# Attention and a gated MLP on one core: products with v per key block, and another set of planner numbers

## The chip, the cores and the metric

The kernel runs on one core of a Trainium2 chip. The metric is the device time of one execution in microseconds (us). Lower is better. The engines are named as in the profile: PE (TensorE; PEld is its weight load), DVE (VectorE), ACT (ScalarE), POOL (GpSimd) and SP (SyncE, which here only issues DMAs).

## The reference

Attention over 8 batches, 8 heads, 576 positions and 64 features per head, with rotary embedding of q and k; then a gated MLP over each batch. All inputs and outputs are float32.

```python
q_rot, k_rot = rotate(q), rotate(k)
scores = (q_rot @ k_rot.T) / sqrt(64)
attn = exp(scores - max(scores)); attn /= sum(attn) + 1e-9
x = heads_joined(attn @ v)                       # (8, 576, 512)
h = relu(x @ w_in)                               # w_in 512 x 1024
u, vv = h[..., :512], h[..., 512:]
vn = (vv - mean(vv)) / sqrt(var(vv) + 1e-6)
vs = w_spatial @ vn + b_spatial                  # w_spatial 576 x 576
out = (u * vs) @ w_out                           # w_out 512 x 512
```

## The kernel before, in words

**The work.** A pair is two heads of one batch; there are 32 pairs, four to a batch. After the fourth pair of a batch, the MLP of that batch is entered. `attention_plain` (pairs 0 to 3) and `attention` (the other 28) have the same steps. For each of nine score tiles, `scores` multiplies on PE into PSUM (tile sc), takes the negated row maximum on DVE (tile nmx, L615) and the exponential with its row sum on ACT (tile e, L617). Two PSUM slots hold the score tiles, so the third tile waits until the exponential of the first has read its slot. `values_plain` and `values` then transpose the exponentials on PE in blocks of 128 keys (tile tp), copy them out of PSUM, and multiply by v into the PSUM tile pv. Pairs 0 to 3 copy plain float32 (tile et, either on ACT at L701 or on DVE at L703) and multiply in float32. From pair 4 on, ACT takes the rounded high part (eh, L645) and DVE the rest (el, L358), and both parts are multiplied. `normalise` takes the reciprocals of the row sums on DVE, sends them through DRAM by DMA (tiles rt and rb), multiplies the output x32 by them, and splits it in a high and a low part (tile x) for the MLP.

**Preparing a pair.** `prepare` loads q and k of a pair (tile st), rotates them (L453, L457), splits them (L446, L449 for q), and copies the parts by DMA into the layouts that the score products read (qs, ks, qz, lk).

**Weights.** The MLP's weights arrive as 64-bit words and `decode` turns each of the 12 blocks of 512 KB into a high and a low float32 part: a DMA, six DVE instructions (L390 twice, L396, L398, L399, L358) and two ACT instructions. `spatial` splits the spatial weights (wsp).

**The MLP.** `mlp` has four products on PE: pa (x by the second half of w_in), pb (x by the first half), pc (the spatial product), pd (the output). pa needs the x of all four pairs of its batch and the blocks wi10 to wi13.

**What sets the order.** Nothing is issued directly. Each instruction, or a few that belong together, is an `op` with an engine, an assumed duration, and a key. `Program.run` plays the program through once, at build time: when an engine is free, it takes the op with the lowest key whose inputs are there and whose buffers (numbered slots) are free. So the keys decide the order on each engine, and on the chip every engine then works through its list in that order; a wait of the first instruction holds up all that stand behind it. `SLOTS` gives three PSUM slots (pm) to the transposed blocks, the decode and the MLP's products together.

- `pair_op` gives an op that POOL can do also to DVE when its key is below `EARLY`. `STEAL` is added to the key on the second engine of an op that has two.
- `UNTIL` is the key up to which ACT, DVE and POOL wait for a more urgent op that will soon be ready.
- `warm` puts a product of zeros on PE (tile warm, a filler) where the plan leaves PE idle. After the planned time `WARM_FULL` (ns) this is done only when PE has been idle for `WARM_AFTER` ns.
- `DEC_V`, `DEC_S`, `DEC_U`, `DEC_O` are the keys of the weight blocks; `PREP_E`, `PREP_AT`, `PLAIN_E`, `PLAIN_AT`, `S_AT2`, `NORM_E` shift the keys of the first six pairs; `MOE0` sets those of the first batch's MLP.

**The products with v of pairs 0 to 3.** `values_plain` has two parts: c = 0 takes three tiles of query rows of both heads, c = 1 the rest. In each there are five key blocks kt. `GROUPS2` says which key blocks share one op on PE: 0 and 1, 2 and 3, then 4 for c = 0; 0 and 1, then 2 to 4 for c = 1.

Of the kernel before, what the change touches and what calls it, by code (L numbers as in the profile page):

```python
# [17 lines left out]
P = 128  # L18
# [18 lines left out]
}  # L37
PSUM = {"sc": 1024, "pv": 512, "pm": 512}
MOE_START, MOE_LENGTH = 92.26, 81.46
DEC_V = [61.0, 61.37, 51.29, 10.34]  # L40
DEC_S = [-41.87, 45.71, 53.32]
DEC_U = [38.89, 69.87, 96.53, 99.39]
DEC_ON = 11.04
DEC_O = [84.23, 50.01, 188.95, 101.97]

CHUNKS = [
# [33 lines left out]
PLAIN_E = [-3.79, 8.57, 7.67, 12.33, 3.82]  # L80
PLAIN_AT = [-3.92, -2.03, -14.17, -18.58]
NORM_E = [42.54, 29.37, 43.65, 15.11, 31.49]
MOE0 = [92.68, 81.44]
# [7 lines left out]
def act_ns(n):  # L91
    return 51 + n * 5 // 6
# [29 lines left out]
class Program:  # L122
# [5 lines left out]
    def op(self, eng, ns, key, f, r=(), w=(), new=(), port=False, late=0):  # L128
        return self.either({eng: ns}, key, lambda e: f(), r, w, new, port, late)
# [139 lines left out]
def tile_attention_gated_mlp(  # L269
# [33 lines left out]
    op = prog.op  # L303
# [251 lines left out]
    def attention_plain(i):  # L555
# [122 lines left out]
    def values_plain(i, c, pieces, pairs_e, e1, vr, x32, key):  # L678

        pv = Buf("pv", None, None, f"pv{i}_{c}")  # L680
        whole_e = [(e, j) for e in pairs_e for j in range(2)] + ([(e1, 0), (e1, 1)] if e1 else [])
        nq = 384 if c == 0 else 192
        K_HI, K_AV, K_HALF = PLAIN_E[2:]
        held = chain[-1:]
        chain.append(f"{i}_{c}")

        def turned(at, name, blocks):

            tp = Buf("pm", None, None, f"tp{name}")
            et = Buf("eh", [P, CW], F32, f"et{name}")  # L690

            def transpose():
                for m, b in enumerate(blocks()):
                    nc.tensor.transpose(out=tp[:, m * P:m * P + P], in_=b, identity=ident)

            n = len(blocks.__defaults__[0])
            op(PE, 110 * n, at, transpose, r=["ident", *whole_e, *([] if name.endswith("_0a") else held)], w=[tp], new=[tp])

            def evacuate(e):
                if e == ACT:  # L700
                    nc.scalar.activation(et[:, :n * P], tp[:, :n * P], AF.Copy)  # L701
                else:
                    nc.vector.tensor_copy(out=et[:, :n * P], in_=tp[:, :n * P])  # L703

            last = [chain[-1]] if name.endswith(f"_{NQ - 1}") else []
            prog.either({ACT: act_ns(n * P), DVE: dve_ns(n * P)}, at + K_HI, evacuate, r=[tp, *held], w=[et, *last], new=[et], port=False)
            return et

        def block(kt):

            at = key + KT_STEP2[c] * kt
            name = f"{i}_{c}_{kt}"
            k0, k1 = kt * P, S + TW + kt * P
            if kt < 4 and c == 0:
                ea = turned(at, name + "a", lambda es=pairs_e, k0=k0: [e[:, k0:k0 + P] for e in es])
                eb = turned(at + 0.1, name + "b", lambda es=pairs_e, k1=k1: [e[:, k1:k1 + P] for e in es])
                return [(ea, 0, 0, P, 0, 384), (eb, 1, 0, P, 0, 384)]
            if kt < 4:
                et = turned(at, name, lambda es=[(pairs_e[0], k0), (e1, k0), (pairs_e[0], k1)]: [e[:, k:k + P] for e, k in es])
                return [(et, 0, 0, P, 0, 192), (et, 1, 0, P, 192, 192)]  # L720
            if c == 0:
                et = turned(at, name, lambda es=pairs_e: [e[:, 4 * P:5 * P] for e in es])
                return [(et, 0, 0, TW, 0, 384), (et, 1, TW, P, 0, 384)]
            et = turned(at, name, lambda es=[pairs_e[0], e1]: [es[0][:, 4 * P:5 * P], es[1][:, 4 * P:]])
            return [(et, 0, 0, TW, 0, 192), (et, 1, TW, P, None, 192)]

        for group in GROUPS2[c]:
            parts = [(kt, *part) for kt in group for part in block(kt)]

            def multiply(parts=parts):  # L730
                for kt, et, h, r0, r1, c0, n in parts:
                    out = pv[64 * h:64 * h + 64, :n]
                    cols = [(out, et[r0:r1, c0:c0 + n])] if c0 is not None else [(out[:, :TW], et[r0:r1, P + TW:2 * P]), (out[:, TW:], et[r0:r1, :P])]
                    for m, (dst, rhs) in enumerate(cols):
                        nc.tensor.matmul(dst, lhsT=vr[r0:r1, kt, h, :], rhs=rhs, start=(kt == 0 and m == 0), stop=(kt == 4 and m == len(cols) - 1))
# [297 lines left out]
```

## Time and profile before

| | |
|---|---|
| runs of the kernel | 953.69, 955.63 and 3209.75 us; median 955.63 us |
| profiled execution | 953.54 us, span 951.7 us |
| busy share of the span | PE 98%, DVE 72%, ACT 79%, POOL 60% |
| PE idle, 0 to 160 us of the span | 14.7 us |
| PE idle, 160 to 280 us | 0.12 us |
| fillers on PE | 71, the last before 110 us |

The run of 3209.75 us is over three times the other two and is not a time of this program's work. The profiled execution agrees with the other two. The shares are means over the whole span: the kernel has a start in which PE waits, and a long part in which it does not.

### The profile page before, as it was taken

Reading aid. Unit: us, or ns where it says so; the run is one execution under the profiler, and the core shown is the slowest. Engines: PE = TensorE matmul, PEld = TensorE weight load, DVE = VectorE, ACT = ScalarE, POOL = GpSimd, SP = SyncE. Lnnn points to the kernel's source line nnn. Section 1 sums busy time; section 2 is a strip of 40 time slices with the busy share of each in tenths; the row PEclk is TensorE's granted clock in tenths of the full one; section 3 lists DMA queues with packets and bytes.
Section 4 is the critical chain, followed back from the end, with each engine's and each line's share of the span. In section 5 each row is a group of like instructions: output and inputs, shape, how many; then the busy total and the mean of one; then the engine's idle time right before and its main releaser. Section 6 shows DMA issues by size and latency. Waiting matters only on the chain.

```text
span 951.7 us, 19634 instructions
## 1 busy us (share of the span) xinstructions
PE 932.9 (98%) x6685; PEld 858.7 (90%) x6685; DVE 683.5 (72%) x1477; ACT 749.9 (79%) x1853; POOL 566.9 (60%) x495
## 2 busy tenths in 40 slices
PE   8999899999999999999999999999999999999998
PEld 4656689999899999999899998999999998999998
DVE  6899887776877678766877668676787767766331
ACT  4989789778987789877897779877898778976452
POOL 7766556655766647776575756656576665752131
PEclk9999999999999999999999999999999999999999
DMA  9787454554454554346355445446544455430101
GB/s 332 228 236 199 131 133 113 139 156 112 122 133 114 160 155 110 103 118 173 115 141 138 99 148 126 122 130 165 126 115 117 128 147 154 103 67 13 64 1 51
DMA packets 57382, 124.65 MB, mean 131 GB/s; under 512 B 13249, under 2 KB 15169, under 8 KB 57282
## 3 DMA queue, kind: packets, MB, share of 16 engines
q1 hardware_dynamic: 56594, 122.73, 47.4%
q8 instruction: 53, 0.87, 0.4%
q10 hardware_dynamic: 688, 0.66, 0.2%
q14 instruction: 47, 0.39, 0.1%
HBM read 66.03 MB, written 9.58 MB: 79 GB/s over the span
## 4 chain that ended last, share of the span: by engine, by line
PE 71%; ACT 12%; DMA 5%; POOL 4%; DVE 3%; issue 3%; SPq 1%; POOLq 0%; DVEq 0%; ACTq 0%
PE pc L849 13%; PE sc L591 12%; PE pv L658 11%; PE pd L867 11%; PE tp L634 10%; PE pb L831 7%; PE pa L808 5%; ACT e L617 3%; ACT eh L645 3%; POOL st L453 2%; SPq L352 1%; DMA vr<-in_v_dram 1%; ACT avt L675 1%; POOL st L457 1%; DMA st<-in_qk_dram 1%
## 5 line engine op out<-in xcount | busy, mean ns | idle before, releaser
L358 DVE TENSOR_TENSOR el<-tp,eh 128x384 fp32r<-128x384 f32 x336 | 185.7, 555 | 128.2 <-ACT eh L645 120.6
L645 ACT ACTIVATE eh<-tp 128x384 fp32r<-128x384 f32 (+1 forms) x504 | 217.2, 433 | 68.2 <-PE tp L634 61.7
L617 ACT ACTIVATE e<-sc,nmx 128x576 f32<-128x576 f32 x288 | 213.1, 741 | 41.5 <-DVE nmx L615 39.1
L615 DVE TENSOR_REDUCE nmx<-sc 128x1 f32<-128x576 f32 x288 | 214.6, 749 | 23.6 <-PE sc L591 18.9
L453 POOL TENSOR_TENSOR st<-st,tabs 128x576 f32<-128x576 f32 x122 | 172.7, 1440 | 70.5 <-DMA st<-in_qk_dram 28.5
L634 PE MATMUL tp<-ident,e 128*128 128x128 f32 (+1 forms) x1176 | 197.8, 273 | 4.2 <-DVE el L358 3.6
L634 PEld LDWEIGHTS tp<-ident,e 128*128 128x128 f32 (+1 forms) x1176 | 146.6, 138 | 17.8 <-DVE el L358 6.3
L658 PE MATMUL pv<-eh,vs 128*128 128x384 f32 (+1 forms) x560 | 147.7, 305 | 0.0
L831 PE MATMUL pb<-x,wi 128*128 128x288 f32 x768 | 145.9, 308 | 0.6 <-DVE el L358 0.2
L849 PE MATMUL pc<-wsp,vn 128*128 128x288 f32 x768 | 145.5, 306 | 0.0
L867 PE MATMUL pd<-g,wo 128*128 128x288 f32 x744 | 138.5, 305 | 0.0
L591 PE MATMUL sc<-ks,qs 128*128 128x288 f32 x620 | 135.6, 308 | 2.4 <-ACT e L617 2.2
L808 PE MATMUL pa<-wi,x 128*128 128x512 f32 x448 | 132.9, 407 | 0.0
L591 PE MATMUL sc<-lk,qz 128*128 128x288 f32 x558 | 119.8, 296 | 0.0
L831 PEld LDWEIGHTS pb<-x,wi 128*128 128x128 f32 x768 | 113.2, 189 | 5.8 <-DVE el L358 2.1
L849 PEld LDWEIGHTS pc<-wsp,vn 128*128 128x128 f32 x768 | 113.2, 189 | 1.2
L658 PE MATMUL pv<-el,vs 128*64 128x384 f32 (+1 forms) x448 | 114.0, 295 | 0.0
L867 PEld LDWEIGHTS pd<-g,wo 128*128 128x128 f32 x744 | 109.6, 189 | 2.2 <-PE pc L849 0.2
L591 PEld LDWEIGHTS sc<-ks,qs 128*128 128x128 f32 x620 | 98.4, 189 | 11.8 <-ACT e L617 6.4
L658 PEld LDWEIGHTS pv<-eh,vs 128*128 128x128 f32 x560 | 98.7, 188 | 4.5
L358 POOL TENSOR_TENSOR g<-u,g 128x288 fp32r<-128x288 f32 x64 | 51.7, 815 | 72.9 <-ACT g L355 72.9
L457 POOL TENSOR_TENSOR st<-st 128x576 f32<-128x576 f32 x62 | 88.6, 1433 | 1.3
(170 smaller groups left out, 1433.0 us busy)
## 6 DMA issues: line engine op xcount, KB each, us to landing
st<-in_qk_dram SPq DMA_DIRECT2D x62, 576.0 KB
ks<-st SPq DMA_DIRECT2D x124, 160.0 KB
qs<-st SPq DMA_DIRECT2D x124, 144.0 KB
vr<-in_v_dram SPq DMA_DIRECT2D x32, 320.0 KB
qz<-st SPq DMA_DIRECT2D x62, 144.0 KB
out_dram<-ob SPq DMA_DIRECT2D x31, 288.0 KB
ws<-in_w_spT_dram SPq DMA_DIRECT2D x2, 576.0 KB
st<-in_qk_dram SPq DMA_DIRECT2D x2, 288.0 KB
```

Of the source, the lines that this page charges most:

```text
L358: eng.tensor_tensor(out=lo, in0=src, in1=hi.bitcast(F32), op=ALU.subtract)
L453: f = lambda e: e.tensor_tensor(out=st[j][:, cols], in0=st[j][:, cols], in1=tabs[:, cols], op=ALU.mult)
L591: nc.tensor.matmul(pt[:, c * 512:c * 512 + HALF], lhsT=lhsT, rhs=rhs[:, k0 + c * HALF:k0 + (c + 1) * HALF], start=(n == 0), stop=(n == len ...
L615: op(DVE, 665, key + k_max, lambda: nc.vector.tensor_reduce(out=nmx.tile, in_=tops(), op=ALU.max, axis=AX.XY, negate=True), r=[pt], w=[nmx ...
L617: op(ACT, 730, key + k_exp, lambda: nc.scalar.activation(e[:, e0:e0 + S].rearrange("p (c n) -> p c n", c=2), tops(), AF.Exp, bias=nmx.tile ...
L634: nc.tensor.transpose(out=tp[:e.shape[1], m * P:m * P + P], in_=e, identity=ident)
L645: nc.scalar.activation(h, p, AF.Copy)
L658: nc.tensor.matmul(pv[0:rows, c1:c2], lhsT=vs[:, kt, h, vp, :], rhs=part[:, c1:c2], start=(kt == 0 and n == 0 and c1 == 0), stop=last)
L808: nc.tensor.matmul(pm.tile, lhsT=lhsT, rhs=win[1, d][:, j, :], start=(d == 0 and n == 0), stop=(d == 3 and n == len(todo) - 1))
L831: nc.tensor.matmul(pm[:, :HALF], lhsT=win[0, d][:, i, f * P:(f + 1) * P], rhs=x[d][:, at:at + HALF], start=(d == 0 and n == 0), stop=(d == ...
L849: nc.tensor.matmul(pm[:, :HALF], lhsT=lhsT, rhs=rhs, start=(t == 0 and n == 0), stop=(t == 4 and n == 1))
L867: nc.tensor.matmul(pm[:, :HALF], lhsT=wout[d,][:, i, m * P:(m + 1) * P], rhs=gs[d][:, at:at + HALF], start=(d == 0 and n == 0), stop=(d == ...
```

## The change

Each key block of `values_plain` becomes an op of its own: `GROUPS2` goes, and the products with v of one kt stand as one entry in PE's list. All keys of the first six pairs, of the weight blocks and of the first MLP are replaced by others, and `EARLY`, `STEAL`, `UNTIL` and the numbers of the fillers too. The instructions of the real work are the same ones: PE has 1176 transposes of the split path, 164 plain transposes and 84 products with v in pairs 0 to 3 in both programs. The fillers go from 71 to 57.

```diff
-DEC_V = [61.0, 61.37, 51.29, 10.34]
+DEC_V = [26.55, 56.08, 48.79, 40.85]
...
-GROUPS2 = [[[0, 1], [2, 3], [4]], [[0, 1], [2, 3, 4]]]
...
-EARLY = 120
-STEAL = 48.41
-WARM_FROM, WARM_FULL, WARM_TO, WARM_NS, WARM_AFTER, WARM_COLS = 2500, 41589.04, 100000, 170, -242.78, 384
+EARLY = 98.54
+STEAL = 18.43
+WARM_FROM, WARM_FULL, WARM_TO, WARM_NS, WARM_AFTER, WARM_COLS = 2500, 32000, 100000, 170, 250, 384
...
-UNTIL = 88.1
+UNTIL = 37.27
...
-PREP_E = [22.66, -9.84, 10.25, 18.9, 53.04, 5.96, 15.45, 5.12, 9.56, -8.37]
-PREP_AT = [-30.48, 14.73, -2.52, -5.21, 7.85, -3.35]
+PREP_E = [27, 8, 8, 9, 9, 11, 30, 8, -2, -9]
+PREP_AT = [0, 0, 0, 0, 0, 0]
...
-        for group in GROUPS2[c]:
-            parts = [(kt, *part) for kt in group for part in block(kt)]
-
-            def multiply(parts=parts):
-                for kt, et, h, r0, r1, c0, n in parts:
+            def multiply(kt=kt, parts=parts):
+                for et, h, r0, r1, c0, n in parts:
...
-            op(PE, len(group) * nq * 39 // 20 + 360, key + KT_STEP2[c] * group[-1] + K_AV, multiply, r=[vr, *dict.fromkeys(part[1] for part in parts)], w=[pv], new=[pv] if group[0] == 0 else [])
+            op(PE, nq * 21 // 11 + 90, at + K_AV, multiply, r=[vr, *dict.fromkeys(p[0] for p in parts)], w=[pv], new=[pv] if kt == 0 else [])
```

The numbers in a row below are the program's buffer names: nmx0_0_1 is the maximum of pair 0, head 0, tile 1, tp1_0_2a a transposed block of pair 1, c = 0, kt = 2; the last number only counts buffers.

The first place is DVE's list at the start: the last steps of rotating q of pair 0 (st0_0) and the first maxima. Before:

```order
L532 SCALAR_TENSOR_TENSOR st0_0_103<-st0_0_103,tabs_63 128x2x384
L615 TENSOR_REDUCE nmx0_0_0_179<-sc0_0_0_153 128x1
L615 TENSOR_REDUCE nmx0_1_0_187<-sc0_1_0_173 128x1
L390 TENSOR_SCALAR dcwi13_200<-wi13raw_155 128x512
L516 TENSOR_TENSOR st0_0_103<-st0_0_103 128x384
L396 SCALAR_TENSOR_TENSOR sgwi13_225<-wi13raw_155,dcwi13_200 128x512
L390 TENSOR_SCALAR dcwi13_200<-wi13raw_155 128x512
L615 TENSOR_REDUCE nmx0_0_1_236<-sc0_0_1_227 128x1
```

And now:

```order
L531 SCALAR_TENSOR_TENSOR st0_0_103<-st0_0_103,tabs_63 128x2x384
L515 TENSOR_TENSOR st0_0_103<-st0_0_103 128x384
L614 TENSOR_REDUCE nmx0_0_0_177<-sc0_0_0_153 128x1
L614 TENSOR_REDUCE nmx0_1_0_185<-sc0_1_0_171 128x1
L452 TENSOR_TENSOR st1_0_134<-st1_0_134,tabs_63 128x576 x2
L614 TENSOR_REDUCE nmx0_0_1_214<-sc0_0_1_205 128x1
```

The addition that ends the rotation of q (L516, now L515) no longer stands behind the first decode step of a weight block; the first decode step of any block (wi10) now comes as row 22 of DVE's list, after seven maxima and two copies.

The second place is DVE's list where pair 4, the first of the split path, begins. Before:

```order
L358 TENSOR_TENSOR wo2_1416<-dcwo2_1299,wo2_1416 128x512
L615 TENSOR_REDUCE nmx4_1_0_1442<-sc4_1_0_1428 128x1
L358 TENSOR_TENSOR el4_0_0_1456<-tp4_0_0_1421,eh4_0_0_1433 128x384
L358 TENSOR_TENSOR el4_0_1_1464<-tp4_0_1_1435,eh4_0_1_1453 128x384
L615 TENSOR_REDUCE nmx4_0_4_1466<-sc4_0_4_1446 128x1
L453 TENSOR_TENSOR st5_1_1334<-st5_1_1334,tabs_63 128x576
L358 TENSOR_TENSOR x3_1477<-x32_3_1323,x3_1477 128x576
L358 TENSOR_TENSOR x3_1477<-x32_3_1323,x3_1477 128x64
L358 TENSOR_TENSOR el4_0_2_1501<-tp4_0_2_1468,eh4_0_2_1489 128x384
L358 TENSOR_TENSOR el4_0_3_1504<-tp4_0_3_1473,eh4_0_3_1493 128x384
```

And now:

```order
L357 TENSOR_TENSOR el4_0_0_1421<-tp4_0_0_1390,eh4_0_0_1405 128x384
L357 TENSOR_TENSOR el4_0_1_1427<-tp4_0_1_1396,eh4_0_1_1409 128x384
L614 TENSOR_REDUCE nmx4_1_1_1435<-sc4_1_1_1411 128x1
L769 TENSOR_TENSOR x32_3_1326<-x32_3_1326,rb3_1360 128x576
L357 TENSOR_TENSOR wo3_1442<-dcwo3_1300,wo3_1442 128x512
L357 TENSOR_TENSOR el4_0_2_1462<-tp4_0_2_1437,eh4_0_2_1450 128x384
L357 TENSOR_TENSOR x3_1464<-x32_3_1326,x3_1464 128x576
L357 TENSOR_TENSOR x3_1464<-x32_3_1326,x3_1464 128x64
L448 SCALAR_TENSOR_TENSOR st6_0_1322<-st6_0_1322 128x576
L357 TENSOR_TENSOR el4_0_3_1492<-tp4_0_3_1466,eh4_0_3_1483 128x384
```

The block el4_0_0 was row 147 of DVE's list, after all 72 decode steps; it is row 140 now, after 65 of them: the last step of wo3 and all six of wo2 come later. Of the work that DVE shares with POOL, st4_0, st5_1, x2, x3 and x4 stood on DVE before; now st1_0, one piece of wsp, x32_3 and x3. The low part of x3 stood ahead of el4_0_2 and stands behind it now; a multiplication of x32_3, which waits for the DMA of rb3, stands ahead of it.

The third place is PE's list in pair 1. Before:

```order
L735 MATMUL pv1_0_660<-et1_0_0a_599,vr1_221 64x384
L735 MATMUL pv1_0_660<-et1_0_0b_606,vr1_221 64x384
L735 MATMUL pv1_0_660<-et1_0_1a_640,vr1_221 64x384
L735 MATMUL pv1_0_660<-et1_0_1b_642,vr1_221 64x384
L694 MATMUL tp1_0_3a_682<-ident_64,e2_1_0_523 128x128
```

And now:

```order
L731 MATMUL pv1_0_602<-et1_0_0a_557,vr1_174 64x384
L731 MATMUL pv1_0_602<-et1_0_0b_567,vr1_174 64x384
L693 MATMUL tp1_0_2a_614<-ident_64,e2_1_0_444 128x128
L693 MATMUL tp1_0_2a_614<-ident_64,e2_1_1_407 128x128
L693 MATMUL tp1_0_2a_614<-ident_64,e2_1_2_472 128x128
L693 MATMUL tp1_0_2b_618<-ident_64,e2_1_0_444 128x128
L693 MATMUL tp1_0_2b_618<-ident_64,e2_1_1_407 128x128
L693 MATMUL tp1_0_2b_618<-ident_64,e2_1_2_472 128x128
L731 MATMUL pv1_0_602<-et1_0_1a_594,vr1_174 64x384
L731 MATMUL pv1_0_602<-et1_0_1b_606,vr1_174 64x384
```

The products with v are cut by transposes after every key block instead of every second one. Over pairs 0 to 3 the unbroken runs of such products go from 20 to 34. From the middle of pair 10 on (its score tile of head 1, tile 0), PE's list is the same in both programs up to the end: the last 2541 rows.

More of the change, by code (lines that the diff above doesn't have):

```diff
@@ L39 @@
 MOE_START, MOE_LENGTH = 92.26, 81.46
-DEC_V = [61.0, 61.37, 51.29, 10.34]
[L41 to L44, printed above, removed]
+DEC_V = [26.55, 56.08, 48.79, 40.85]
+DEC_S = [13.58, 17.95, 35.36]
+DEC_U = [60.17, 42.39, 60.35, 107.48]
+DEC_ON = 6.04
+DEC_O = [78.92, 112.46, 208.15, 120.91]
 CHUNKS = [
@@ L60 @@
 ]
-S_AT2 = [[0.99, 10.82, -7.22, 13.5, 0.81, 1.57], [19.07, 23.53, 32.12]]
-GROUPS2 = [[[0, 1], [2, 3], [4]], [[0, 1], [2, 3, 4]]]
-KT_STEP2 = [2.15, 2.61]
-VALUES_AT2 = [10.98, 25.07]
-EARLY = 120
-STEAL = 48.41
-WARM_FROM, WARM_FULL, WARM_TO, WARM_NS, WARM_AFTER, WARM_COLS = 2500, 41589.04, 100000, 170, -242.78, 384
+S_AT2 = [[1.7, 4.65, -0.43, 6.89, 3.7, 8.06], [10.81, 19.68, 16.79]]
+KT_STEP2 = [1.84, 0.43]
+VALUES_AT2 = [13.48, 26.26]
+EARLY = 98.54
+STEAL = 18.43
+WARM_FROM, WARM_FULL, WARM_TO, WARM_NS, WARM_AFTER, WARM_COLS = 2500, 32000, 100000, 170, 250, 384
 PATIENT = (DVE, ACT, POOL)
-UNTIL = 88.1
+UNTIL = 37.27
 LATE_LOAD = 2200
@@ L77 @@
 PREP = [30.19, 35.32, -8.17, -24.92, 16.24, 1.9, 50.58, 22.5, 37.15, -9.46]
-PREP_E = [22.66, -9.84, 10.25, 18.9, 53.04, 5.96, 15.45, 5.12, 9.56, -8.37]
-PREP_AT = [-30.48, 14.73, -2.52, -5.21, 7.85, -3.35]
[L80 to L83, printed above, removed]
+PREP_E = [27, 8, 8, 9, 9, 11, 30, 8, -2, -9]
+PREP_AT = [0, 0, 0, 0, 0, 0]
+PLAIN_E = [1.25, 4, 1.0, 4.0, 3.0]
+PLAIN_AT = [0, 0, 0, 0]
+NORM_E = [15, 21, 26, 24, 27]
+MOE0 = [90, 82]
 K_NORM, K_RELU, K_GATE, K_GHI, K_GLO, K_OB, K_OUT = 28.57, -7.71, 10.98, 19.59, 15.51, -9.41, -27.84
@@ L707, in turned @@
             return et
-        def block(kt):
+        for kt in range(NQ):
             at = key + KT_STEP2[c] * kt
@@ L716, in block @@
                 eb = turned(at + 0.1, name + "b", lambda es=pairs_e, k1=k1: [e[:, k1:k1 + P] for e in es])
-                return [(ea, 0, 0, P, 0, 384), (eb, 1, 0, P, 0, 384)]
-            if kt < 4:
+                parts = [(ea, 0, 0, P, 0, 384), (eb, 1, 0, P, 0, 384)]
+            elif kt < 4:
                 et = turned(at, name, lambda es=[(pairs_e[0], k0), (e1, k0), (pairs_e[0], k1)]: [e[:, k:k + P] for e, k in es])
-                return [(et, 0, 0, P, 0, 192), (et, 1, 0, P, 192, 192)]
-            if c == 0:
+                parts = [(et, 0, 0, P, 0, 192), (et, 1, 0, P, 192, 192)]
+            elif c == 0:
                 et = turned(at, name, lambda es=pairs_e: [e[:, 4 * P:5 * P] for e in es])
-                return [(et, 0, 0, TW, 0, 384), (et, 1, TW, P, 0, 384)]
-            et = turned(at, name, lambda es=[pairs_e[0], e1]: [es[0][:, 4 * P:5 * P], es[1][:, 4 * P:]])
-            return [(et, 0, 0, TW, 0, 192), (et, 1, TW, P, None, 192)]
-        for group in GROUPS2[c]:
-            parts = [(kt, *part) for kt in group for part in block(kt)]
-            def multiply(parts=parts):
-                for kt, et, h, r0, r1, c0, n in parts:
+                parts = [(et, 0, 0, TW, 0, 384), (et, 1, TW, P, 0, 384)]
+            else:
+                et = turned(at, name, lambda es=[pairs_e[0], e1]: [es[0][:, 4 * P:5 * P], es[1][:, 4 * P:]])
+                parts = [(et, 0, 0, TW, 0, 192), (et, 1, TW, P, None, 192)]
+            def multiply(kt=kt, parts=parts):
+                for et, h, r0, r1, c0, n in parts:
                     out = pv[64 * h:64 * h + 64, :n]
```

## The prediction

> **What bounds the kernel now.** I read the page's head first, then the windows of the span, then the fillers alone.
>
> ```profile
> span 951.7 us, 19634 instructions
> PE 932.9 (98%) x6685; PEld 858.7 (90%) x6685; DVE 683.5 (72%) x1477; ACT 749.9 (79%) x1853; POOL 566.9 (60%) x495
> ```
>
> PE is busy for 98%, but this mean covers two stages. The windows give, for each stretch, its length, the busy time of PE, PEld, DVE, ACT and POOL, PE's granted clock, and the DMA share:
>
> ```profile
> 0.00:30.00 30.00, 25.76 (x124) 13.75 (x124) 20.57 (x34) 15.73 (x36) 19.12 (x30) 1.00 0.87 297
> 30.00:103.67 73.67, 67.62 (x466) 46.25 (x467) 69.95 (x113) 67.08 (x165) 50.40 (x42) 1.00 0.79 225
> 103.67:107.60 3.93, 3.83 (x24) 2.97 (x22) 3.75 (x6) 3.56 (x10) 3.71 (x4) 1.00 0.88 272
> 107.60:111.00 3.40, 0.00 (x0) 0.00 (x0) 3.40 (x4) 0.00 (x0) 3.40 (x3) 0.99 0.02 3
> 111.00:114.00 3.00, 2.91 (x12) 2.69 (x13) 2.20 (x6) 1.50 (x4) 0.85 (x1) 0.50 0.00 0
> 114.00:137.80 23.80, 23.60 (x147) 20.55 (x146) 20.61 (x55) 20.62 (x54) 11.26 (x9) 0.99 0.45 115
> 137.80:160.00 22.20, 21.62 (x162) 20.17 (x162) 18.00 (x41) 21.00 (x54) 15.87 (x13) 1.00 0.58 146
> 160.00:280.00 120.00, 119.88 (x882) 114.44 (x881) 87.54 (x192) 99.01 (x247) 76.25 (x65) 1.00 0.47 124
> 280.00:952.00 672.00, 667.70 (x4879) 637.89 (x4877) 457.46 (x1032) 521.41 (x1292) 386.08 (x335) 1.00 0.43 115
> ```
>
> From 160 to 280 us PE is idle for 0.12 us: it is the bound. Both programs share their order from the middle of pair 10 on; 1666 matmuls stand ahead of that point, and the windows up to 280 us count 1817. So the change can move the end only by what it does to the start. There PE is idle for 4.24 + 6.05 + 0.10 + 3.40 + 0.09 + 0.20 + 0.58 = 14.7 us, and DVE for only 3.7 us of the 73.67 up to 103.67: DVE sets the pace there (95% busy), with ACT behind it (91%).
>
> ```profile
> 0.00:30.00 30.00, 12.26 (x55) 1.00 0.87 297
> 30.00:110.00 80.00, 5.23 (x16) 1.00 0.77 221
> ```
>
> These are the fillers alone: 55 before 30 us, 16 after. All work on PE is the same after the change, so the time is the span less what the start loses. A gain of 2% would be 19 us. The start offers 14.7 us of idle time plus the fillers, and most of the first 14 us is waiting for the first data, so I rule a gain of that size out almost wholly.
>
> **The first score tiles.** Rows of DVE, PE and, from the chain of waits, a DMA:
>
> ```profile
> 8.76 0.95 DVE L532 SCALAR_TENSOR_TENSOR st<-st,tabs 128x768 f32<-128x768 f32 x1
> 12.42 0.69 DVE L390 TENSOR_SCALAR dcwi<-wi13raw 128x512 int32<-128x512 int32 x1 [1.01 <-PE warm L941]
> 13.02 0.89 DVE L516 TENSOR_TENSOR st<-st 128x384 f32<-128x384 f32 x1
> 22.04 0.76 DVE L615 TENSOR_REDUCE nmx<-sc 128x1 f32<-128x576 f32 x1 [0.56 <-PE sc L601]
> 103.67 0.55 DVE L358 TENSOR_TENSOR el<-tp,eh 128x384 fp32r<-128x384 f32 x1
> 9.20 1.24 PE L601 MATMUL sc<-kf,st 64*128 64x288 f32 x6
> 10.37 2.61 PE L941 MATMUL warm<-zero 128*128 128x384 bf16 x15
> 14.06 2.18 PE L601 MATMUL sc<-kf,st 64*128 64x288 f32 x8 [1.08 <-DVE st L516]
> 4.83 7.49 DMA wi13raw<-in_w_in_dram
> ```
>
> Weight block wi13 lands at 4.83 + 7.49 = 12.32 us. The decode step L390 waits for it, and the addition L516 stands behind that step though its own input was there at 8.76 + 0.95 = 9.71. PE's third score tile waits for L516 and begins at 14.06. After the change the addition comes directly behind L532 and ends near 10.6. PE then has its second tile (until 9.20 + 1.24 = 10.44) and nine fillers of 2.61 / 15 = 0.174 us in front of the third: 10.44 + 1.57 = 12.0. That is 2 us sooner.
>
> **DVE's list up to pair 4.** The row at 22.04 is the seventh maximum; el4_0_0 begins at 103.67. Between them stand 123 rows of the order (24 to 146), so one takes 81.63 / 123 = 0.664 us, waits included. Afterwards seven maxima are done by row 19, 2 us sooner (20.0), then two copies, then rows 22 to 139: 118 rows. Prices of one maximum, decode step and copy:
>
> ```profile
> L615 DVE TENSOR_REDUCE nmx<-sc 128x1 f32<-128x576 f32 x35 | 25.8, 752 | 2.8 <-PE sc L591 1.4 <-PE sc L601 1.1
> L399 DVE SCALAR_TENSOR_TENSOR dcwi<-dcwi,sgwi 128x512 f32<-128x512 f32 x7 | 4.9, 693 | 0.1
> L703 DVE COPY et<-tp 128x384 f32<-128x384 f32 x3 | 1.6, 547 | 0.0
> ```
>
> Maximum and copies end at 20.0 + 0.75 + 1.1 = 21.9; with 118 x 0.664 = 78.4 el4_0_0 begins near 100.3: a gain of 3.4 us. This holds if DVE stays the bound at the same pace. ACT has to do nearly the same number of rows before it (154 for 156) and was idle for 6.6 us of 73.67, so it allows the gain. The ends are 0 (the score tiles' two PSUM slots or ACT set the pace) and 7.1 (DVE's 3.7 us of waiting go as well).
>
> **The key blocks.** PE's rows for two key blocks of pair 0:
>
> ```profile
> 27.41 0.54 PE L735 MATMUL pv<-et_0a,vr 128*64 128x384 f32 x1
> 28.43 0.48 PE L735 MATMUL pv<-et_1a,vr 128*64 128x384 f32 x1
> 28.85 0.55 PE L694 MATMUL tp_3a<-ident,e 128*128 128x128 f32 x3
> ```
>
> From the first product to the next transposes it is 1.44 us; the four steps between are 0.37, 0.32, 0.34 and 0.42, so a run costs 4 x 0.32 plus 0.16 for going in and out. Fourteen more runs cost 14 x 0.16 = 2.2 us on PE, in a stretch where PE has 6.05 us idle and 16 fillers. That cover hides most of it; I take 0.7 (a third), ends 0 and 2.2. The gain of an earlier start of these products I put at nothing, since the copies, not the products, are waited for there.
>
> **The hole at 107.6 us.** DVE, POOL and PE in order of time:
>
> ```profile
> 105.54 1.81 DVE L453 TENSOR_TENSOR st<-st,tabs 128x576 f32<-128x576 f32 x1
> 107.28 3.29 DVE L358 TENSOR_TENSOR x<-x,x 128x576 fp32r<-128x576 f32 x2
> 110.49 1.01 DVE L358 TENSOR_TENSOR el<-tp,eh 128x384 fp32r<-128x384 f32 x2
> 105.31 3.30 POOL L453 TENSOR_TENSOR st<-st,tabs 128x576 f32<-128x576 f32 x2
> 108.57 3.28 POOL L457 TENSOR_TENSOR st<-st 128x576 f32<-128x576 f32 x2
> 111.09 0.69 PE L634 MATMUL tp<-ident,e 128*128 128x128 f32 x2 [3.59 <-DVE el L358]
> 68.59 0.75 DVE L453 TENSOR_TENSOR st<-st,tabs 128x576 f32<-128x576 f32 x1
> 89.65 1.16 DVE L358 TENSOR_TENSOR x<-x,x 128x576 fp32r<-128x576 f32 x2
> ```
>
> PE stops for 3.59 us because el4_0_2 stands behind st5_1 and x3 on DVE, and these took 1.81 and 3.29 us beside POOL where the same forms took 0.75 and 1.16 elsewhere. Then the clock is 0.50 for 3 us, which costs 1.5 more. The hole costs 5.1 us in all. So a collision with POOL added 1.06 and 2.13 us.
>
> After the change st5_1 is not DVE's, and x3 stands behind el4_0_2; a multiplication of x32_3 stands ahead of it, which costs 0.75 alone and waits for rb3. So the hole gets smaller; by how much depends on where POOL is. Ends: 5.1 saved, or 0. I take the middle, 2.6.
>
> **The fillers.** Fourteen fewer, nine of them before the first transposes of pair 0, take 14 x 0.174 = 2.4 us off PE, where PE was waiting anyway: nothing for the sum. The row at 14.06 us has a gap of 1.08 us in a window with the clock at 1.00, and the gap of 3.40 is followed by 0.50; what lies between, no row shows. [...]
>
> **What was put off.** Seven decode steps come after el4_0_0 now, 7 x 0.69 = 4.8 us. From 103.67 to 137.80 DVE is busy for 3.75 + 3.40 + 2.20 + 20.61 = 29.96 of 34.13 us, so 4.2 us idle, and part of what is put off fits there. I take half on the path, 2.4; ends 0 and 4.8. Behind 137.8 us PE has the MLP's products beside the attention, and DVE 4.2 us of 22.2 free; I put nothing there.
>
> **The sum.** Against the profiled execution, 953.54 us: -3.4 + 0.7 - 2.6 + 2.4 = -2.9, so 950.6. The undisturbed runs, 953.69 and 955.63, lie 1.1 above the profiled one on average, which gives 951.7; I forecast 952. The ends are 953.54 - 7.1 - 5.1 = 941.3 and 953.54 + 2.2 + 4.8 = 960.5.
>
> **Rivals**, on the profiled execution's scale.
>
> - *The debt comes back.* The put-off decode steps all fall on the path and the hole stays: -3.4 + 0.7 + 0 + 4.8 = +2.1, 955.6. For it: DVE is the bound up to 103.67 and 88% busy behind. Against: 4.2 us of free time, and none of the steps is needed before the first output product.
> - *A longer hole, slower than before.* DVE's row for x32_3 waits for a DMA and for ACT's copy of the last product, and el4_0_2 stands behind it. If POOL collides with x32_3 and x3, 1.06 + 2.13 = 3.2 us come on top of the present hole, and the debt of 4.8 follows: -3.4 + 2.2 + 3.2 + 4.8 = +6.8, 960.3. For it: POOL is busy for 3.71 of 3.93 us just ahead of the hole. Against: x3 stands behind el4_0_2 now. It decides from the point where el4_0_2 is over 3.6 us late, the hole of today.
> - *The clock falls at the start.* With nine fillers fewer, a gap between 12 and 30 us grows to 3.4 us and about 3 us run at half clock: 950.6 + 1.5 = 952.1. Against: the longest gap there is 1.08 us, and the nine taken out are 1.6 us together.
> - *The order does not carry over.* The score tiles of pair 0 go at the pace of their two slots, not of DVE's list, and later waits eat the 2 us: nothing changes, 953.5 to 955.
>
> **Chances.** The forecast 0.43, the debt 0.25, the longer hole 0.17, the clock 0.05, no effect 0.10. The range, 944 to 961, holds all these cases and the upper end of the sum; of the lower end, with all gains at once, it leaves out 3 us. About a fifth is left for holes that no row shows. Within 2% (about what a measurement of this kernel can tell from no change) are all five; slower by more needs over 19 us of new idle time, several holes with the slow clock: 0.04. Faster by more: 0.01.
>
> **What the profile after would show.** The third score tile near 12.0 instead of 14.06, the first el near 100.3, no PE gap over 3 us and no clock of 0.50 between 100 and 115 us, PE busy with 57 fillers, and DVE busier between 100 and 140. A PE gap of over 3.4 us in pairs 0 to 4, or the first el later than 103.7, would make the forecast wrong.

## The result, and the profile after

The changed kernel takes 947.67 us (median of 8 runs, 946.99 to 951.0), the kernel before 955.2 us beside it: ratio 0.9925, 95% interval 0.9901 to 0.9948. The forecast was 952, range 944 to 961, within 2%. The gain is real and lies inside the range, but it is 7.5 us where 2.9 were reckoned, so some terms of the sum were wrong. The profiled execution took 947.33 us, with a span of 945.6 where before had 951.7.

The head of the page after, and the same windows as before (length, busy time of PE, PEld, DVE, ACT and POOL, PE's clock, DMA share, GB/s):

```profile
span 945.6 us, 19600 instructions
PE 933.7 (99%) x6671; PEld 855.3 (90%) x6671; DVE 675.9 (71%) x1475; ACT 748.5 (79%) x1853; POOL 564.3 (60%) x497
```

```profile
0.00:30.00 30.00, 27.48 (x132) 14.79 (x134) 20.46 (x32) 16.99 (x36) 19.05 (x29) 1.00 0.86 278
30.00:103.67 73.67, 69.50 (x458) 44.77 (x457) 68.63 (x113) 66.43 (x169) 55.47 (x48) 1.00 0.81 241
103.67:107.60 3.93, 3.93 (x23) 3.11 (x22) 3.13 (x7) 3.78 (x10) 0.00 (x0) 1.00 0.78 214
107.60:111.00 3.40, 3.40 (x20) 2.91 (x20) 3.29 (x7) 1.98 (x5) 1.69 (x2) 1.00 0.52 115
111.00:114.00 3.00, 2.83 (x21) 2.36 (x19) 2.97 (x10) 2.84 (x9) 0.00 (x0) 1.00 0.90 201
114.00:137.80 23.80, 22.99 (x148) 20.26 (x148) 22.00 (x56) 21.58 (x53) 15.49 (x12) 1.00 0.39 107
137.80:160.00 22.20, 22.20 (x174) 21.48 (x173) 14.31 (x37) 19.65 (x53) 13.92 (x12) 1.00 0.35 96
```

From 107.6 to 111 us PE is busy for all of 3.40 us where it stood still, and the next 3 us run at full clock instead of 0.50. PE's busy time over the whole span is nearly the same (933.7 and 932.9): the gain is idle time of PE, and it lies ahead of 160 us, where the windows leave 2.52 + 4.17 + 0.17 + 0.81 = 7.7 us idle for 14.7 before.

Three rows split it: the first el of pair 4 on DVE, the first pb product on PE, and the end. After (rows of DVE, then of PE, in order of time):

```profile
13.73 0.76 DVE L614 TENSOR_REDUCE nmx<-sc 128x1 f32<-128x576 f32 x1 [0.26 <-PE sc L600]
30.50 0.68 DVE L389 TENSOR_SCALAR dcwi<-wi13raw 128x512 int32<-128x512 int32 x1
101.41 1.01 DVE L357 TENSOR_TENSOR el<-tp,eh 128x384 fp32r<-128x384 f32 x2
103.00 0.90 DVE L769 TENSOR_TENSOR x<-x,rb 128x576 f32<-128x576 f32 x1
105.85 0.90 DVE L357 TENSOR_TENSOR x<-x,x 128x576 fp32r<-128x576 f32 x2 [0.52 <-ACT x L354]
12.45 2.20 PE L600 MATMUL sc<-kf,st 64*128 64x288 f32 x8 [0.25 <-ACT e L616]
132.22 0.57 PE L827 MATMUL pb<-x,wi 128*128 128x288 f32 x3
```

Before:

```profile
137.80 0.56 PE L831 MATMUL pb<-x,wi 128*128 128x288 f32 x3
```

| stretch of the span | before | after | difference | forecast |
|---|---|---|---|---|
| start to el4_0_0 | 103.67 | 101.41 | -2.26 | -3.4 + 0.7 = -2.7 |
| el4_0_0 to the first pb | 34.13 | 30.81 | -3.32 | -2.6 + 2.4 = -0.2 |
| the first pb to the end | 813.9 | 813.4 | -0.5 | 0 |
| sum | 951.7 | 945.6 | -6.1 | -2.9 |

The multiplication of x32_3 took 0.90 us, and so did the two steps of x3's low part, which took 3.29 before with POOL at work beside all of it: POOL has no work at all from 103.67 to 107.60 now (0.00 us, for 3.71), so the collision with it is gone. The row of the hole, el4_0_0 to the first pb, holds most of the gain. The rest of the 7.5 us between the medians (7.5 - 6.1 = 1.4) is not in these two profiles: the profiled execution of before lies 1.7 us under its median, that of after 0.3 us. Such differences between executions of one kernel go with the clock, as the list below shows.

Each of these executions has a mean clock that PE was granted. Pooled over the batches of the experiments for the kernel before, and over the two batches of the changed kernel, these are the executions (below, "at full clock" means a mean of 0.999 or more):

```
kernel   executions   at clock 0.999 or 1.000     at a lower clock
before   96           6:  952.35 to 953.03        90: 953.47 to 964.07, median 955.1
after    18           11: 946.81 to 948.28        7:  950.68 to 953.12, median 951.7
```

At full clock the medians are 952.5 and 947.5, so the change is worth 5.0 us there. Before, nearly every execution lost clock besides; after, seven of 18 do. Two things are to be explained: the 5 us, and why some executions after are 4 us longer.

### The profile page after: what moved, and what is told of

Read it like the earlier page. It is cut to its first block, busy times and chain, and to the rows that moved or that the text cites. A ratio compares the mean times of both kernels' runs of the same rounds, so it can differ in the third digit from the quotient of the medians.

```text
span 945.6 us, 19600 instructions
## 1 busy us (share of the span) xinstructions
PE 933.7 (99%) x6671; PEld 855.3 (90%) x6671; DVE 675.9 (71%) x1475; ACT 748.5 (79%) x1853; POOL 564.3 (60%) x497
## 4 chain that ended last, share of the span: by engine, by line
PE 75%; ACT 11%; DMA 5%; DVE 3%; POOL 3%; issue 2%; SPq 1%; POOLq 0%; DVEq 0%; ACTq 0%
PE pc L845 13%; PE sc L590 13%; PE pv L657 11%; PE pd L863 11%; PE tp L633 10%; PE pb L827 9%; PE pa L804 5%; ACT e L616 3%; ACT eh L644 2%; DMA st<-in_qk_dram 2%; PE pv L731 2%; POOL st L452 1%; SPq L351 1%; POOL st L456 1%; DVE nmx L614 1%
```

## The experiments

Each experiment takes the finished order of one of the two kernels, moves a few instructions in it, and issues it. In the diffs `move(first, ops)` puts `ops` right ahead of `first`. Line numbers of these kernels are some 14 to 25 higher, since the moves stand ahead.

**The hole closed.** On the kernel before:

```diff
+ st5_1 times the tables: POOL instead of DVE
+ move(eh4_0_4's copy, [x3's low part])     # behind el4_0_2 and el4_0_3
```

> The kernel before, with two moves that close the hole at 107.6 us and nothing else: the multiplication st5_1 goes from DVE to POOL, and the low part of x3 stands behind el4_0_2 and el4_0_3 instead of ahead of them. Theory (the hole costs PE's stall of 3.59 us and 1.5 us for the clock of 0.50 behind it, and all of it comes off the end): 955.2 - 5.1 = 950.1, ratio 0.9947, no clock below 0.95 from 107 to 115 us. Rival 1 (half of it, as the prediction took): 952.6, ratio 0.9973. Rival 2 (what is put behind the products is waited for next, the gain is given back): 954 to 956.

**Half of it.** Only the first of the two lines:

> The kernel before, with the first of the two moves alone: st5_1's multiplication on POOL, x3 still ahead of el4_0_2 on DVE. If the order is what matters, x3 meets POOL's work as it did (3.29 us) and only st5_1's 1.81 us go: PE's stall falls from 3.59 to about 1.8 us, and if the clock follows the length of the stall it does not fall: 955.2 - 1.8 - 1.5 = 951.9, ratio 0.9965. If the collision is what matters, x3 goes back to about 1.2 us and the stall is gone: 950.1, ratio 0.9947. If POOL's longer work only collides longer, the stall stays over 3 us with the clock at 0.50 behind it: 955, ratio 1.000.

**The start alone.** On the kernel before:

```diff
+ move(first maximum, [end of q's rotation, L516])
+ drop six of the fifteen fillers ahead of the third score tile
```

> The kernel before, with the start alone: the addition that ends the rotation of q stands ahead of the decode step of wi13 on DVE, and nine fillers instead of fifteen stand ahead of the third score tile. The third score tile begins near 12.2 instead of 14.06. Theory (DVE's list is the pace up to pair 4, so an earlier start goes through to the end): el4_0_0 near 101.7, 955.2 - 2.0 = 953.2, ratio 0.9979. Rival (later waits, for weight blocks or score slots, eat the 2 us before pair 4): el4_0_0 at 103.5 to 104, 955, ratio 1.000.

**Both.** The three edits together:

> The kernel before, with the moves of the closed hole and of the early start together, and the products of the key blocks and all else as before. If the two gains add: 955.2 - 5.1 - 2.0 = 948.1, ratio 0.9926, which is all of what the whole change brought (947.67, ratio 0.9925). If the start's 2 us are eaten: 950.1, ratio 0.9947. If the earlier start brings DVE's list up against POOL's at another place (a new hole): 951 to 955.

| kernel | median | ratio, 95% interval | at full clock | el4_0_0 | el4_0_0 to pb |
|---|---|---|---|---|---|
| hole closed | 952.52 | 0.9975 (0.9956 to 0.9994) | 949.8 (3 of 12) | 110.00 | 30.19 |
| only st5_1 moved | 950.62 | 0.9961 (0.9947 to 0.9975) | 950.3 (8 of 11) | 103.75 | 30.86 |
| start alone | 955.55 | 1.0008 (0.9986 to 1.003) | 951.9 (2 of 12) | 102.83 | 35.16 |
| both | 951.91 | 0.9968 (0.9952 to 0.9984) | 949.0 (2 of 12) | 105.65 | 30.19 |

The last two columns are from the one profiled execution. (Of these, the hole closed and both had the clock halved near 16 and 10 us, for 13.66 and 6.83 us, which is why el4_0_0 comes so late there.) With the hole closed, the stretch behind el4_0_0 falls from 34.13 to 30.19, by 3.9 us; with st5_1 moved alone by 3.3. That kernel, DVE, then POOL, then PE:

```profile
106.19 2.60 DVE L375 TENSOR_TENSOR x<-x,x 128x576 fp32r<-128x576 f32 x2 [0.48 <-ACT x L372]
105.41 4.67 POOL L470 TENSOR_TENSOR st<-st,tabs 128x576 f32<-128x576 f32 x3
109.31 0.44 PE L651 MATMUL tp<-ident,e 128*128 128x128 f32 x2 [1.73 <-DVE el L375]
```

x3 still meets POOL's work (2.60 us), but el4_0_2 comes 1.8 us sooner, PE waits 1.73 instead of 3.59 us, and the clock stays at 1.00. So what was expected of the order holds: half the stall and none of the clock's fall, which is most of the gain of the closed hole. At full clock both kernels gain 2 to 3 us (952.5 to 949.8 and 950.3), not the 5.1 that the theory gave: the clock's share of the 5.1 is not in executions at full clock, and the two profiles with x3 moved have a new wait of PE of 1.11 us behind it (at 117.43 and 113.07). Why nine of 12 executions with the hole closed lost clock and only three of 11 with st5_1 moved alone, no run settled.

The start alone brought nothing, and its trace says why (PE, then DVE in order of time):

```profile
11.80 2.20 PE L620 MATMUL sc<-kf,st 64*128 64x288 f32 x8
12.05 0.69 DVE L409 TENSOR_SCALAR dcwi<-wi13raw 128x512 int32<-128x512 int32 x1 [0.59 <-DMA wi13raw<-in_w_in_dram]
14.79 0.75 DVE L634 TENSOR_REDUCE nmx<-sc 128x1 f32<-128x576 f32 x1
102.83 0.55 DVE L377 TENSOR_TENSOR el<-tp,eh 128x384 fp32r<-128x384 f32 x1
```

The third score tile begins 2.26 us sooner, but its maximum stands behind the decode of wi13 and begins only 0.5 us sooner (14.79 for 15.30); el4_0_0 comes 0.84 us sooner. In the changed kernel that decode stands at 30.50 us, and the maximum begins at 13.73. The hole, still there, then ate the 0.84: the clock fell for longer (below).

Both edits together bring 952.5 - 949.0 = 3.5 of the 5.0 us at full clock. For the 1.5 us that are left, the profiles offer el4_0_0, at 101.41 in the changed kernel and at 102.83 with the start alone: the maximum begins 1.06 us sooner with the decode of wi13 out of its way. No run moved that decode, so this is a reading and not a test.

**Is DVE's list the pace?** On the kernel with the hole closed:

```diff
+ drop four of the six decode steps of wo2 on DVE
```

> The kernel with the hole closed, and four of DVE's six decode steps of wo2 left out (one block of output weights is then not decoded), 4 x 0.69 = 2.8 us of DVE work ahead of el4_0_0. It tests what the term of the start rests on. If DVE's list sets the pace up to pair 4, el4_0_0 comes 2.8 us sooner after the third score tile (86.8 us where the kernel before has 103.67 - 14.06 = 89.6) and the end too: near 950.3 - 2.8 = 947.5 at full clock. If ACT or PE sets it, el4_0_0 comes 0 to 1 us sooner: 949.5 to 950.3. The prediction's put-off steps were costed by the same pace.

Here one block of output weights is not decoded. The median was 957.28 us, ratio 0.9995 (0.9959 to 1.0031). Its profile and that of the closed hole had the same slow spell of 13.66 us near 16 us, so the two can be laid side by side. Closed hole, PE and DVE:

```profile
14.03 2.17 PE L619 MATMUL sc<-kf,st 64*128 64x288 f32 x8 [1.07 <-ACT dcwi L413]
110.00 0.55 DVE L376 TENSOR_TENSOR el<-tp,eh 128x384 fp32r<-128x384 f32 x1
```

Four steps out, PE and DVE:

```profile
14.21 2.18 PE L621 MATMUL sc<-kf,st 64*128 64x288 f32 x8 [0.96 <-DVE st L536]
107.31 0.76 DVE L635 TENSOR_REDUCE nmx<-sc 128x1 f32<-128x576 f32 x1 [0.75 <-PE sc L611]
110.21 1.01 DVE L378 TENSOR_TENSOR el<-tp,eh 128x384 fp32r<-128x384 f32 x2
114.34 3.40 DVE L378 TENSOR_TENSOR x<-x,x 128x576 fp32r<-128x576 f32 x2
```

From the third score tile to el4_0_0 it is 95.97 us in the one and 96.00 in the other. 2.8 us of DVE work taken out bring nothing; DVE waits for score tiles instead. So DVE, busy for 66.20 of the 71 us from 30 to 101 with the hole closed (93%), did not set the pace of that stretch in the last 10 us, where the four steps stood; for the rest of it this run says nothing. (The end came later: x3 took 3.40 us where it took 2.12 with the hole closed, PE waited 0.88 us for it, and 3.4 us of half clock followed.)

**The key blocks and the fillers.** The changed kernel was run once more, then with joined key blocks, then without fillers:

> The changed kernel once more, beside the two that follow. The earlier executions of the kernels show times that go with the mean granted clock: 946.99 to 947.81 at 0.999 to 1.000, 950.68 and 951.0 at 0.998 and 0.996. Theory (what spreads the times is how long the clock is halved early on, and the changed kernel offers few occasions): most executions at 947 to 948 with the clock at 0.999 or above, about one in four at 950 to 951. Rival (the spread has nothing to do with the clock): times of 950 and more at a clock of 1.000.

```diff
+ pairs 0 to 3: move(product with the last block of a run, [those of the one or two blocks ahead])
```

> The changed kernel with the products of two or three neighbouring key blocks of pairs 0 to 3 joined into one run again, as in the kernel before, and nothing else moved. By the prediction's price (0.16 us of a run, a third of it on the path) 947.7 - 0.7 = 947.0. If every run costs PE in full: 947.7 - 2.2 = 945.5 or less. If the time between the products is covered by waiting, or joined products come too late for the copies behind them: 947.5 to 949.

```diff
+ drop all fillers but the first 18
```

> The changed kernel without its fillers behind 7 us: the first 18 stay, the other 39 are left out. Their places become gaps of up to about 2 us between 8 and 26 us and of 0.2 to 0.9 us in pairs 2 and 3; no gap is as long as 3.4 us. [...] By the traces of the closed hole and of both moves, where the clock went to 0.50 behind gaps of 1.05 and 1.67 us, it falls in most executions for 3 to 14 us near the start: median 949 to 954, clock 0.993 to 0.998.

| kernel | median | ratio, 95% interval | at full clock |
|---|---|---|---|
| changed kernel again | 949.53 | 0.9931 (0.9899 to 0.9963) | 947.7 (5 of 10) |
| key blocks joined | 951.21 | 0.9941 (0.9914 to 0.9968) | 948.3 (1 of 10) |
| no fillers behind 7 us | 951.53 | 0.9958 (0.993 to 0.9986) | none of 10 |

Joining the blocks gained nothing in the median. Without the fillers the clock was 0.987 to 0.992 in every one of ten executions, and the median lies 4.0 us above what the changed kernel takes at full clock (947.5). In the profile the longest gap of PE between 2 us and the first fall is 0.99 us:

```profile
5.95:9.36 3.41, 2.01 (x10) 1.00 1.07 400
9.36:26.44 17.08, 15.86 (x43) 0.50 0.90 284
```

Not all of the 4.0 us is the fillers' part. The ten executions form two groups, 949.29 to 950.31 and 952.75 to 954.33, and the profile, from the upper one, also has the wait for a load that comes next. The lower group has a median of 949.92, so the fillers are worth nearer 2.4 us.

The second run of the changed kernel gave half of its executions over 950 us, more than the one in four expected, all with a clock below 0.999, and its profile fell among them. SP, then ACT, then PE, and PE's windows around it:

```profile
79.93 0.33 SPq L351 DMA_DIRECT2D vr<-in_v_dram  x1
86.83 0.74 ACT L354 ACTIVATE vs<-vr 128x640 fp32r<-128x640 f32 x1 [2.65 <-DMA vr<-in_v_dram]
89.05 0.90 PE L693 MATMUL tp_1b<-ident,e 128*128 128x128 f32 x3 [3.48 <-ACT et_1a L700]
```

```profile
84.91:88.32 3.41, 0.66 (x4) 1.00 0.86 186
88.32:91.74 3.42, 2.68 (x11) 0.50 0.34 79
```

This is a hole that the prediction did not see. ACT splits v of pair 4 (vs4) and waits 2.65 us for its load; the copies of pair 3 stand behind it; PE waits 3.48 us, and from 88.32 us on the clock is 0.50 for 6.83 us. The profiles with joined blocks and without fillers have the same wait of ACT:

```profile
85.86 0.74 ACT L376 ACTIVATE vs<-vr 128x640 fp32r<-128x640 f32 x1 [2.39 <-DMA vr<-in_v_dram]
88.17 0.74 ACT L372 ACTIVATE vs<-vr 128x640 fp32r<-128x640 f32 x1 [1.73 <-DMA vr<-in_v_dram]
```

PE waited 4.02 and 2.56 us there, and the clock was 0.50 for 6.83 and 3.41 us behind it. So three of the four profiles with vs4 and its load at this place show the wait, and the first profile of the changed kernel alone does not. In the kernel before, the same load and the same step of ACT are 7.0 us apart:

```profile
84.99 0.33 SPq L352 DMA_DIRECT2D vr<-in_v_dram  x1
92.03 0.73 ACT L355 ACTIVATE vs<-vr 128x640 fp32r<-128x640 f32 x1
```

In the first profile of the changed kernel they are:

```profile
79.64 0.33 SPq L351 DMA_DIRECT2D vr<-in_v_dram  x1
83.77 0.76 ACT L354 ACTIVATE vs<-vr 128x640 fp32r<-128x640 f32 x1
```

Only 4.1 us are left, in a stretch in which the DMA engines have become full. Two windows of that stretch before (ACT's busy time, PE's clock, DMA share, GB/s):

```profile
82.00:84.00 2.00, 2.00 (x6) 1.00 0.40 150
84.00:86.00 2.00, 2.00 (x7) 1.00 0.09 17
```

And after:

```profile
82.00:84.00 2.00, 2.00 (x6) 1.00 1.02 347
84.00:86.00 2.00, 2.00 (x5) 1.00 0.98 213
```

In the first profile the load came in time, in the second it did not. Two ways to test that: let vs4 come later, or let its load go first.

```diff
+ move(et3_0_3a, [vs4's high part])                  # ACT, 5 us later
+ move(vr5's load, [vs4's low part])                 # POOL
+ move(et3_1_4, [vs5's high part]);  move(st6's first step, [vs5's low part]);  move(vr7's load, [vr6's load])
```

> The changed kernel with one thing moved: ACT's and POOL's steps that split v of pairs 4 and 5 (vs4, vs5) stand 5 to 6 us later, and the loads of vr5 and vr6 that wait for them follow; pair 4 needs vs4 only from 101 us on. In the second profile of the changed kernel ACT stood 2.65 us at vs4 for the load of vr4, PE then 3.48 us, and the clock was 0.50 for 6 us behind it; in the first profile the load came in time. Theory (this late load is what splits the times of the changed kernel into 946.8 to 948.3 and 950.7 to 953.1): the upper group goes, nearly all executions at 946.5 to 948.5 with the clock at 0.999 to 1.000, ratio to the kernel before 0.991 to 0.993. Rival 1 (the slower half has other causes, such as the clock at the start): the upper group stays, median 948 to 951. Rival 2 (ACT's and POOL's later places are as bad): all of it 948 to 951.

```diff
+ move(wo1's load, [vr4's load])
```

> The changed kernel with the load of vr4 ahead of the 512 KB load of wo1 in SP's queue, and nothing else moved. The load of vr4 was issued 79.64 and 79.93 us into the two profiles and waited for the last product with vr2; wo1's was issued 2.7 us ahead of it. If wo1's data in the DMA engines hold up vr4, it lands up to 2 us sooner, ACT's wait at vs4 stays under 1 us and the upper group of times goes: median 947 to 948. If other transfers or the load's own time (4 to 7 us from issue to use) set it, the upper group stays: median 948 to 951, about half of the executions over 950.

With the steps later: median 948.56 us, ratio 0.9919 (0.9888 to 0.9951); three of six executions at 947.6 to 947.9 and full clock, one at 949.23, two still at 951.0 and 951.7. The one at 949.23 was profiled: the longest wait of PE from 80 to 95 us is 0.59, and its clock fell at 8.5 us, for 3.41 us, behind a wait of 1.82 us at the first score tiles. So the clock at the start slows some executions too, as the first rival said. With the load first: 952.88 us, 0.9957 (0.9938 to 0.9975), none of 12 at full clock. In its profile vs4 does not wait, and another transfer does the harm:

```profile
92.63 0.82 PE L606 MATMUL sc<-ks,qs 128*128 128x288 f32 x2 [3.78 <-DMA qz<-st]
```

The edit did not bring the load forward: it was issued at 79.45 us (79.64 in the changed kernel), since SP has to wait for the last product with vr2 first. Only wo1's load, now behind it, came 2.9 us later. The DMA share from 78 to 80 us fell to 0.09 (0.81 in the changed kernel), and from 84 to 90 it was 0.99 to 1.03. So this run does not test whether wo1's data hold up vr4; it shows what an issue that waits does to the transfers behind it. The steps later take the wait at vs4 away, and the last two runs build on that. The first also fills the dip in the queue (DMA share 0.51 and 0.81 from 76 to 80 us); the second joins the key blocks again:

```diff
+ the three lines of the later vs4 and vs5
+ move(vr4's load, [wo3's load])
```

> The kernel with the steps of vs4 and vs5 later, and the 512 KB load of wo3 moved ahead of vr4's load in SP's queue, where SP stands 2 to 3 us for the last product with vr2. There the DMA engines are 0.51 and 0.81 busy (76 to 80 us of the changed kernel), behind it 0.97 to 1.02 (82 to 86). Theory (what waits in this stretch is whichever transfer comes last in a full queue; filling the dip relieves the later ones): no PE wait over 1.5 us from 80 to 95 us, nearly all executions at 946.5 to 948.5, ratio 0.991 to 0.992. Rival 1 (vr4's load, now behind 512 KB more, comes too late even for the later steps): PE waits of 2 us and more near 88 us, median 950 to 952. Rival 2 (the slower executions that are left come from the clock at the start, not from transfers): as with the later steps alone, 947.6 to 951.7 with a third of them over 950.

```diff
+ the three lines of the later vs4 and vs5
+ pairs 0 to 3: joined key blocks
```

> The kernel with the steps of vs4 and vs5 later, and the products of neighbouring key blocks of pairs 0 to 3 joined into runs of two or three as before the change. It asks for the price of the key blocks where no late load covers it. In the profile with joined blocks alone the first transposes of pair 3 began at 81.84 where the changed kernel has 82.27, its first score tile 0.14 us later: 0.5 us for the joining. If that goes through to the end: 947.7 - 0.5 = 947.2, ratio 0.9914. If each of the runs saved counts in full: 945.5, ratio 0.990. If a wait eats it, or the later product is waited for: 947.7 to 948.5.

The first gave 947.53 us, all five executions from 946.84 to 949.14, four of them at full clock; ratio 0.9925 (0.9901 to 0.995). Its profile has a span of 945.1 us, no slow spell, no wait of PE over 0.59 us from 80 to 95. It is no faster than the changed kernel is at full clock (947.5); what it seems to bring is that hardly an execution misses that. With 7 of 18 executions over 950 after the change, none of five would happen by chance in one case of twelve (0.61 to the fifth), so this points that way and settles nothing. With joined key blocks it was 949.87 us, 0.9944 (0.9923 to 0.9964), none of nine at full clock; its profile shows why:

```profile
83.80:87.22 3.42, 1.75 (x11) 1.00 0.99 228
87.22:90.62 3.40, 3.40 (x11) 0.50 0.89 207
85.82 0.55 PE L718 MATMUL tp_1b<-ident,e 128*128 128x128 f32 x3 [1.39 <-ACT et_1a L725]
```

A wait of 1.39 us for the copies of pair 3, and 3.4 us of half clock behind it. With the steps later and the blocks apart, the same row waits 0.59:

```profile
87.11 0.55 PE L713 MATMUL tp_1b<-ident,e 128*128 128x128 f32 x3 [0.59 <-ACT et_1a L720]
```

There the products of the first key block stand between tp_1a and tp_1b and fill the wait; joined, they come behind tp_2b. Both runs with joined blocks were slower in the median than the run they build on by 1.3 to 1.7 us, though the intervals overlap. The clock tells more: 18 of 19 executions with joined blocks lost clock, and 10 of 24 of the two kernels they build on. So apart, the blocks cost nothing that these runs can see, and they seem to keep the clock up.

## Why the prediction was right, and where it was not

**The class and the range** held because the argument on the bound held: PE is full from 160 us on (busy for 119.88 of the 120 us to 280 before, for 119.98 after), so no more than the start's idle time could move. The range was 17 us wide for a gain of 2.9, so that it held says little of the terms. From the first pb to the end it is 812.9 to 814.7 us in all fourteen profiles.

**The hole** was sized wrong: "I take the middle, 2.6". It closed, by the moves that its mechanism named (st5_1 off DVE, x3 behind el4_0_2, x32_3 without a collision, at 0.90 us). The two profiles with both moves put it at 3.9 us of the stretch behind el4_0_0. Its second half, 1.5 us for the clock, was right for the one profile it was read from, and is a matter of chance in others: six of 96 executions of the kernel before show no lost clock.

**What was put off** was sized wrong too: 2.4 taken. The changed kernel needs 30.81 us from el4_0_0 to pb, the kernels with the hole closed and nothing put off 30.19: 0.6 us. That DVE's free time took the rest, as the argument against the debt said it might, fits and was not tested. These two terms are 1.3 + 1.8 of the 3.2 us by which the sum missed the profiles' difference.

**The start** came out near (2.26 for 3.4), and its working failed. The step was "this holds if DVE stays the bound at the same pace", 118 rows by 0.664 us. The run with four steps out shows that DVE's rows of the last 10 us did not set el4_0_0, and the start alone shows that the earlier tile is worth 0.84 us while the decode of wi13 stays ahead of the maxima. From the third score tile to el4_0_0 the changed kernel needs 88.96 us, the kernel before 89.61: 1.61 us of the 2.26 are the earlier tile, 0.65 the rest. What sets that pace (ACT's copies, the score tiles, both) no run settled.

**The key blocks** (+0.7): not seen; joining them was no gain in two runs. The step that failed is "the gain of an earlier start of these products I put at nothing, since the copies, not the products, are waited for there": just because the copies are waited for, a product that stands ahead of the wait fills a part of it (0.59 us of it are left, for 1.39).

**The fillers** (0): right for the fourteen taken out, as far as the 11 executions at full clock show. The rival of the clock was priced at 1.5 us and a chance of 0.05, on the ground that no gap grows to 3.4 us, the length of the hole before (3.40). The run without fillers shows that ground to be wrong: there the clock fell with no gap over 0.99 us. The chance was low for another reason too: the five add up to 1.00, so the fifth that the prediction keeps for holes that no row shows is not in them.

**The rival of a longer hole** was placed at x32_3 and did not come there. Its like came 20 us earlier, at vs4, in one of the two profiles of the changed kernel: a load with 4.1 us from its issue to its reader where it had 7.0. There PE stood for 3.48 us in pair 3, which is the prediction's own sign of being wrong (a gap of over 3.4 us in pairs 0 to 4); the median held because most executions escaped it. The prediction listed what moved on DVE, PE and POOL, and costed no transfer behind the first score tiles. That is the place where it would have shown.

**The resolution** was set too wide. The prediction took 2% as about what a measurement can tell from no change; here the interval, 0.9901 to 0.9948, tells 0.75% from none.

## What to carry to other kernels

Where PE is the bound later on, what a new order is worth is what it does to the few waits of PE in the start; and a wait can cost more than its length, since the clock may fall behind it (to 0.50 for 3.42 us behind the 3.59 of the hole before). In these profiles half clock followed each of the six waits of PE of 2.5 us and more in pairs 0 to 4; of those of 1 to 2 us it followed some (1.39, 1.67, 1.82) and not others (1.73, 1.85, 1.97). When steps move forward, look at the slack of each load that feeds them, from its issue to its reader, and at the DMA share in that stretch: the load of vr4, with 4.1 us and a share of 0.98 to 1.02, came in time in one execution and left ACT waiting for 2.65 us in another, and one profile shows only one of the two. A short product that stands ahead of a wait is worth more there than behind it (PE waited 0.59 us behind the first key block's products, 1.39 with them joined). An engine that is 93% busy need not set the pace; taking out a few of its steps tells (2.8 us of DVE's work out, and 96.00 us for 95.97).

## What the runs showed of the hardware

In these profiles the clock fell to 0.50 and rose to 1.00 in steps of one length. The slow spells lasted 3.4 us (five), 6.8 (five), 13.66 (two) and 17.08 (one): 1, 2, 4 and 5 times 3.41. Two profiles have two spells each: the falls are at 16.40 and 118.80 us with four steps out, at 9.36 and 91.28 without fillers, so 102.40 and 81.92 us apart, 30 and 24 times 3.413. Nor did each fall come behind an idle stretch of that length. Here are the 3.41 us ahead of the fall and the spell, in the kernel before, where the same hole cost one step:

```profile
107.51:110.92 3.41, 0.00 (x0) 1.00 0.02 5
110.92:114.34 3.42, 3.25 (x13) 0.50 0.00 0
```

in the start alone, where nearly the same wait (3.60 us) fell otherwise on the steps and cost two:

```profile
105.57:108.98 3.41, 1.11 (x6) 1.00 0.18 38
108.98:112.39 3.41, 2.11 (x9) 0.50 0.00 0
112.39:115.80 3.41, 3.41 (x13) 0.50 0.00 0
```

and with the hole closed, at the start:

```profile
13.09:16.50 3.41, 2.47 (x11) 1.00 1.02 417
16.50:30.16 13.66, 13.66 (x35) 0.50 0.66 222
```

PE was busy for 2.47 of the 3.41 us ahead of that fall, and then busy without a gap for four steps before the clock rose (with four steps out, where the spell is as long, three groups of four score products of 64*128 took 2.29 us each of it, 1.24 at full clock). The order up to there is the same in the kernel before, whose profile has no fall at that place. Counted back from its own fall at 110.92 us, 28 steps of 3.413, the step there is this one:

```profile
11.94:15.35 3.41, 2.33 (x13) 1.00 1.02 410
```

With less PE work than the 2.47 us above, the clock stayed, so PE's busy time alone does not draw the border, if the steps keep their places in this profile as they do in the two with two spells. In the rows above, steps with 0.00, 0.66, 1.11, 1.75, 2.01 and 2.47 us of PE work were followed by a fall, and the first three of the four full steps with the hole closed by no rise. One kernel's times spread over 2 to 12 us (2.3 with wo3's load earlier, 11.7 for the kernel before); that the steps fall elsewhere in each execution would fit this and was not shown. What draws the border, and whether score tiles of 64*128 have a part in it, was not tried.
